# A linear-attention and SwiGLU kernel: making a third block's basis weights in block 1 beside the weights, and a later block's attention by halves of the heads

## The chip, the cores and the metric

The kernel runs on one core of a Trainium2 chip. The core has five engines that run side by side and meet at semaphores: TensorE (PE, matrix products into PSUM; its weight loads are listed as PEld), VectorE (DVE), ScalarE (ACT), GpSimd (POOL) and SyncE (SP, which here only issues DMAs). The metric is the device time in microseconds (us). Each engine works through its own list of instructions in a fixed order; an instruction that waits holds up all behind it on its engine.

## The reference

q, k and v have 8 batches, 8 heads, 576 positions and 64 columns in float32.

```python
kv  = einsum('bhsd,bhse->bhde', k, v)          # no softmax
out = einsum('bhsd,bhde->bhse', q, kv)
rms = sqrt(mean(out*out, axis=-1) + 1e-6)
x   = (out / rms * g_norm)                     # -> 4608 tokens x 512
g   = x @ w_gate                               # 512 x 1536
h   = g * (1 / (1 + exp(-g))) * (x @ w_val)
y   = h @ w_out                                # 1536 x 512
```

## The kernel before, in words

**Blocks.** The 4608 tokens are cut into nine blocks of 512. A block crosses from one batch to the next, since a batch has 576 positions. Block 0 is computed plainly while the weights come in. Blocks 1 and 2 run alone, with a scheme of seven products in place of eight (Winograd's form of Strassen's). Blocks 3 to 8 run in three pairs with the scheme applied twice, so that each weight tile of a pair is replaced by 7 x 7 basis blocks ("leaves") of 128 x 128. These are kept in the DRAM tensor `w` and streamed back for each pair.

**Products.** An up-projection of blocks 1 and 2 has six units (`Up`, index j), each with the products 1, 5, 6, 2, 7, 4, 3. They are called (j, p) here. Unit j runs (j,1), (j,5), then the last two of the unit before, (j-1,4) and (j-1,3), then (j,6), (j,2), (j,7). Each is eight instructions at L650 in the trace. Products 1, 6, 7 and 4 accumulate in one PSUM tile `b`, 5 and 3 in `c`, 2 in `a`. After 1, 6 and 7 ScalarE copies `b` out (L666, L670, L700). After 2, 7 and 3 VectorE adds `a` or `c` to such a copy (L696, L704, L717, listed at L130); (j,3) writes into `c` and so comes after the add of (j,7). GpSimd makes the operand tiles `t` (L131) and multiplies into `h` (L132), and VectorE makes sums of `h` (`h_sums`). The down-projection (`Down`) then runs the products in the order 1, 6, 5, 7, 2, 4, 3 with 24 instructions each.

**Leaves.** In block 1 the three tiles that GpSimd made for a unit are turned into leaves (`leaf_steps`, L908): per tile four VectorE operations and two sends to `w` by SP (L915). The other four outer tiles, that is the raw weights `wg[j]` and `wv[j]`, are turned into leaves in block 2, two groups of tiles per unit with four VectorE operations and two sends each. This is done in place, so it can only begin after the unit's last product, at `p == 3`; the last unit's are done in block 2's down-projection (`latest`, L1091). `make` (L1043) runs up to four such steps after each product in block 1 and two in block 2.

**Attention ahead.** While block 2 is computed, block 3's attention is made beside its products, and block 4's is begun (`ahead`, L1209). A pair (j, p) names the product after which a step is placed:

- (0,7): the k^T v products of block 3 (`visit`; L368), into two PSUM tiles `m`. Block 3's q loads are queued (32 DMAs at L331, sent five after each product), and half of block 4's k and v loads (L310).
- (1,7): half of block 4's k^T v. Then VectorE transposes q (`turn_q`, L384), in two operations.
- (2,5) and (3,5): the products q (k^T v) of one half of block 3 each (`heads`, L423), into the two tiles `m`. A half is two of the four tiles of tokens, with all heads, and so it needs both transposed halves of q, since a transposed half has half of the heads. Behind each half come ScalarE's squares, VectorE's sums and root, and VectorE's scaling (L132), which frees `m`. At (2,5) block 4's q loads are queued.
- (3,7): the second half of block 4's k^T v. At (4,5) sixteen DMAs move the transposed x into its place (`place_x`, L511, eight by SP and eight by ScalarE's queue); at (5,1) ScalarE multiplies it by the gain (`gain_x`, L518); at (5,5) VectorE makes four sums of x (`sum_steps`).

**What sets the order.** A scheduler at build time orders each engine's list. In block 2, PE's list and, in the up-projection, VectorE's are held in program order (`in_order`, L1284 and L1309); ScalarE's, GpSimd's and SP's are not, except that the sends of leaves stay in order. DMAs share eight completion counters in turn, and each waits for the one before it on its counter, whichever queue that was on. A tile pool's buffer is given out again when all that used it are done: four buffers for loads (`ld`), five for `r`, nine for `t`, two for `m`.

Of the kernel before, what the change touches and what calls it, by code (L numbers as in the profile page):

```python
# [8 lines left out]
F32 = mybir.dt.float32  # L9
# [5 lines left out]
P = 128  # L15
# [3 lines left out]
def kernel(  # L19
# [41 lines left out]
    nc = tc.nc  # L61

    B, H, S, D = q.shape
# [166 lines left out]
    class Att:  # L230


        def __init__(self, n):
            self.n = n

            self.cut, half = divmod(n, 2)
            self.split = half * D
            self.ps, self.z = {}, None
            self.q, self.k, self.v, self.room = [], {}, {}, None
            self.halves = []  # L240
            self.quarters = n > 0
            slot = (n - PAIRED) % 2
            self.x, self.xi = (x_alone, xi_alone) if n < PAIRED else (x_slots[slot], xi_slots[slot])
            self.homes = {}
# [160 lines left out]
        def chores(self, i):  # L405
# [5 lines left out]
            for u in range(2):  # L411
                yield lambda u=u: self.scale(i, (u,))

        def heads(self, i, pairs, pools=None):
            if pools:
                self.ps[i] = [pool.tile([P, 2, NS, D], F32, name=pool.name[0]) for pool in pools]
            for t in range(2):
                for j in pairs:
                    for b, _, p0, p1 in self.parts(2 * i + t):
                        for p in range(p0, p1, D):  # L420
                            for u in range(2):
                                rows = slice(u * D, (u + 1) * D)
                                self.multiplied = nc.tensor.matmul(  # L423
                                    self.ps[i][u][p : p + D, t, j, :],
                                    lhsT=self.qt[rows, 2 * i + t, j, p : p + D], rhs=kvs[b % 3][rows, j, :],
                                    start=True, stop=True,
                                )

        def squares(self, i, us=(0, 1)):
            if self.z is None or 0 < self.n < TURNED:  # L430
                self.z = st_pool.tile([P, 2, 2, 2, NS], F32, name="z")
            if i == 0 and us[0] == 0:
                self.sq = self.place("sq").rearrange("p f (t j d) -> p f t j d", t=2, j=NS)
# [16 lines left out]
        def guess(self, i, k):  # L450

            z = self.z[:, i : i + k]
            nc.vector.tensor_scalar(out=z, in0=z, scalar1=1.0 / D, scalar2=eps, op0=OP.mult, op1=OP.add)
            self.y, a = (st_pool.tile([P, 2, 2, 2, NS], F32, name=x) for x in "ya")
# [15 lines left out]
        def scale(self, i, us=(0, 1)):  # L470
            if i == 0 and us[0] == 0:
                self.xts = self.place("xts").rearrange("p (i t) (j u d) -> p i t j u d", i=2, j=NS, u=2)
            for u in us:
                y = self.y[:, i, u].unsqueeze(3).to_broadcast([P, 2, NS, D])
                self.scaled = mul(nc.vector, self.xts[:, i, :, :, u], self.ps[i][u], y)

        def turn_x(self, i):
            xt = self.xts[:, i].rearrange("p t j u d -> p t j (u d)")
# [193 lines left out]
    class Up(Quad):  # L672
# [51 lines left out]
        def multiply(self, p):  # L724
            super().multiply(p)
            ffn = self.ffn
            if ffn.n == 1:
                if p == 5:
                    self.leaf_room = ring().rearrange("p f (s c) -> p (f s) c", c=P)
                if p in (5, 7, 4):  # L730
                    at = 3 * (5, 7, 4).index(p)
                    ffn.making.extend(leaf_steps(self.j, [(self.w[p].unsqueeze(1), (p,))], self.leaf_room[:, at:]))
            if ffn.n == 2 and p == 3:
                room = xi_alone.rearrange("p a b c -> p (a b) c")
                halves = lambda t: t[self.j].rearrange("p (o i) c -> p o i c", o=2)
                steps = leaf_steps(self.j, [(halves(wg), (1, 2)), (halves(wv), (6, 3))], room)
                if self.j < NP - 1:
                    ffn.making.extend(steps)
                else:
                    ffn.latest.extend(steps)  # L740

    class Inner:

# [159 lines left out]
    def t_tile(key=None):  # L903

        stream.held.append(key)
        return t_pool.tile([P, 2, 2 * P], F32, name="t")

    def leaf_steps(j, sources, room):  # L908


        i = 0

        def send(os, ps, src):
            dst = stream.dram[:, j, steps_of(OUTERS, os), steps_of(INNERS, ps)].rearrange("p o i c -> p o (i c)")
            tc.keep_in_program_order(nc.sync.dma_start(out=dst, in_=src))  # L915

        for t, os in sources:
            n = len(os)
            t = t.rearrange("p o i (e c) -> p o i e c", e=2)
            b11, t2_, b22 = t[:, :, 0, 0], t[:, :, 0, 1], t[:, :, 1, 1]  # L920
            to = room[:, i : i + 3 * n].rearrange("p (o r) c -> p o r c", r=3)
            yield lambda b22=b22, t2_=t2_: sub(nc.vector, t2_, b22, t2_)
            yield lambda b11=b11, t2_=t2_: add(nc.vector, t2_, t2_, b11)
            yield lambda t=t, t2_=t2_, to=to, n=n: sub(
                nc.vector, to[:, :, 1:3], t[:, :, 1], t2_.unsqueeze(2).to_broadcast([P, n, 2, P])
            )
            yield lambda t=t, os=os: send(os, (1, 6, 2, 3), t.rearrange("p o i e c -> p o (i e c)"))
            yield lambda b11=b11, t2_=t2_, to=to: sub(nc.vector, to[:, :, 0], b11, t2_)
            yield lambda to=to, os=os: send(os, (7, 4, 5), to.rearrange("p o r c -> p o (r c)"))
            i += 3 * n  # L930

    class Down(Quad):
        def __init__(self, ffn):
# [87 lines left out]
    class Ffn:  # L1021
        def __init__(self, n, att):
            self.n, self.att = n, att
            self.h = h_alone if n < PAIRED else h_slots[(n - PAIRED) % 2]
            self.ps, self.leaf_room, self.ended, self.owed = {}, None, None, None

            self.making, self.latest = [], []
            self.chores, self.sends = [], []
            self.visited = None

# [11 lines left out]

        def make(self, count):  # L1043
            for _ in range(count):
                if self.making:
                    self.making.pop(0)()

        def up(self, fill):

# [4 lines left out]
            for i, this in enumerate(units):  # L1054
                if i + 1 < len(units):
                    units[i + 1].prepare()
                for unit, p in this.sequence(last):
                    if unit:
                        visited, self.visited = self.visited, None
                        with tc.issue_after(visited.ins) if visited else ExitStack():  # L1060
                            unit.multiply(p)
                        self.make(4 if self.n == 1 else 2)
# [11 lines left out]
        def down(self, nxt, then={}):  # L1074
# [3 lines left out]
            for p in (1, 6, 5, 7, 2, 4, 3) if 5 in fill else (1, 5, 6, 7, 2, 4, 3):  # L1078
# [9 lines left out]
                    fill[p]()  # L1088
                if p in then:
                    then[p]()  # L1090
                if p == 5 and self.latest:  # L1091

                    with tc.issue_after(nxt.scaled.ins), tc.issue_after(nxt.placed.ins):
                        for step in self.latest:
                            step()
                if p == 1:

# [110 lines left out]

    def ahead(ffn, att, then):  # L1209

        def load(att):
            for i in range(2):
                ffn.sends += att.quarter_steps(i, (0, 1), (nc.sync,))

        def visits():
            visit(ffn, att, (0, 1))
            load(att)
            then.load_kv(0)

        def turn():  # L1220
            visit(ffn, then, (0,), True)
            ffn.chores += [lambda: att.turn_q(0), lambda: att.turn_q(1), lambda: then.load_kv(1)]

        def half(i):
            with tc.issue_after(ffn.multiplied.ins):
# [3 lines left out]
            if i:  # L1229
                ffn.chores += att.turn_steps()  # L1230

        def last():
            visit(ffn, then, (1,), True)
# [138 lines left out]
```

## Time and profile before

| | us |
|---|---|
| median of 3 runs | 1032.51 |
| lowest, highest | 1031.76, 1033.65 |
| the profiled execution | 1033.4 |
| its span on the core | 1031.6 |
| PE busy | 1000.9 (97% of the span) |
| DVE, POOL, ACT busy | 653.2, 366.0, 232.5 |
| block 1, up-projection, from | 155.9 to 232.3 |
| block 2, up-projection, from | 269.9 to 369.0 |

Times in rows of the profile are from the start of the span. A row of the timeline gives start, duration, engine, line, operation, what is written and read, the count, and in brackets how long the engine stood idle before it and what ended that. A row of PE's waits gives the engine and what it waited to do, whose result it waited for, the total, how often, and the longest. The line L130, L131 or L132 is that of a small helper for adding, subtracting or multiplying, so that such rows are told apart by their tiles. "Granted clock" is TensorE's clock as a share of its full speed.

### The profile page before, as it was taken

The page shows a single profiled execution, that of the slowest core. Times are in us where ns is not written, and L with a number is a line of the kernel's source. Part 1 is how long each engine was busy: PE and PEld are TensorE (multiplying, and loading weights), DVE is VectorE, ACT ScalarE, POOL GpSimd, SP SyncE. Part 2 cuts the span into 40 slices and gives each one's busy share as a digit, 9 for nine tenths or more (in the row PEclk, how much of TensorE's full clock was granted, in tenths as well). Part 3 has the DMA queues.
Part 4 walks back from the last instruction along what each step waited for, and adds up shares of the span by engine and source line. Part 5 has one row for each costly group of instructions (what it writes and reads, how often), then busy time and mean ns, then how long its engine had stood idle before and what let it go on. Part 6 is the DMA issues. An engine that isn't in the chain of part 4 may idle for free.

```text
span 1031.6 us, 17068 instructions
## 1 busy us (share of the span) xinstructions
PE 1000.9 (97%) x6506; PEld 835.1 (81%) x6506; DVE 653.2 (63%) x1118; ACT 232.5 (23%) x367; POOL 366.0 (35%) x290
## 2 busy tenths in 40 slices
PE   5999999999968999999999999999999999999998
PEld 4544688888857888888888888888888888888887
DVE  2999685664348697666666755666777566666211
ACT  2766112221212221111211212212112122121100
POOL 0000262527224140444565102555651026546600
PEclk9999999999989899999999999999999999999999
DMA  8689643463166668586752364667412654543011
GB/s 216 200 263 266 131 79 110 135 202 71 59 158 164 170 171 237 143 236 155 167 148 53 101 144 148 164 168 181 112 22 61 143 146 148 156 142 100 1 42 41
DMA packets 247763, 143.23 MB, mean 139 GB/s; under 512 B 149121, under 2 KB 226945, under 8 KB 247681
## 3 DMA queue, kind: packets, MB, share of 16 engines
q1 hardware_dynamic: 212736, 137.67, 49.1%
q10 hardware_dynamic: 34880, 4.46, 2.7%
q8 instruction: 52, 0.85, 0.4%
q14 instruction: 31, 0.25, 0.1%
q0 software_dynamic: 64, 0.00, 0.0%
HBM read 104.99 MB, written 28.70 MB: 130 GB/s over the span
## 4 chain that ended last, share of the span: by engine, by line
PE 90%; DMA 3%; DVE 2%; SPq 2%; ACT 1%; issue 1%; POOL 1%; ACTq 0%; DVEq 0%; POOLq 0%
PE b L650 24%; PE b L801 21%; PE c L650 11%; PE c L801 11%; PE a L650 6%; PE a L801 5%; PE b L1110 4%; PE c L1110 4%; PE m L423 2%; PE m L368 1%; SPq L331 1%; DMA arena<-in_v_dram 1%; POOL t L131 1%; DMA arena<-r 1%; DMA ld<-in_v_dram 1%
## 5 line engine op out<-in xcount | busy, mean ns | idle before, releaser
L801 PE MATMUL b<-arena,t 128*128 128x256 f32 x1008 | 244.5, 381 | 0.0
L801 PEld LDWEIGHTS b<-arena,t 128*128 128x128 f32 x1008 | 190.0, 190 | 29.6 <-DVE r L130 2.4
L130 POOL TENSOR_TENSOR r<-r 128x256 f32<-128x256 f32 (+1 forms) x90 | 94.7, 1053 | 247.1 <-DMA t<-w 150.1
L130 DVE TENSOR_TENSOR r<-c,r 128x512 f32<-128x512 f32 (+1 forms) x170 | 104.8, 625 | 114.9 <-PE c L801 40.9
L130 DVE TENSOR_TENSOR r<-b,r 128x512 f32<-128x512 f32 (+1 forms) x234 | 139.0, 607 | 60.8 <-PE b L801 55.4
L132 POOL TENSOR_TENSOR arena<-r 128x1024 f32<-128x1024 f32 (+1 forms) x54 | 102.0, 1904 | 108.1 <-DVE r L130 64.2
L131 POOL TENSOR_TENSOR t<-wo 128x512 f32<-128x512 f32 x54 | 75.8, 1424 | 181.2 <-DVE wo L130 105.5
L130 DVE TENSOR_TENSOR r<-a,r 128x512 f32<-128x512 f32 x93 | 59.3, 638 | 122.9 <-PE a L650 87.4
L801 PE MATMUL c<-arena,t 128*128 128x256 f32 x504 | 122.5, 379 | 0.8 <-ACT r L815 0.8
L131 DVE TENSOR_TENSOR arena<-arena 128x512 f32<-128x512 f32 (+3 forms) x102 | 100.9, 998 | 15.1 <-PE b L650 13.8
L801 PEld LDWEIGHTS c<-arena,t 128*128 128x128 f32 x504 | 95.6, 190 | 14.5 <-ACT r L815 1.2
L650 PE MATMUL b<-wo,arena 128*128 128x256 f32 x432 | 98.0, 381 | 0.1
L650 PE MATMUL b<-t,arena 128*128 128x256 f32 x432 | 96.4, 379 | 1.4 <-POOL s L130 0.7
L650 PEld LDWEIGHTS b<-t,arena 128*128 128x128 f32 x432 | 81.9, 190 | 13.2 <-POOL s L130 1.1
L650 PEld LDWEIGHTS b<-wo,arena 128*128 128x128 f32 x432 | 81.3, 190 | 12.0 <-DVE arena L132 0.9
L815 ACT COPY r<-b 128x512 f32<-128x512 f32 x54 | 31.7, 586 | 191.3 <-PE b L801 191.3
L131 POOL TENSOR_TENSOR t<-arena 128x512 f32<-128x512 f32 x36 | 48.8, 1366 | 68.6 <-PE b L650 26.4
L801 PE MATMUL a<-arena,t 128*128 128x256 f32 x252 | 66.1, 379 | 0.0
L801 PEld LDWEIGHTS a<-arena,t 128*128 128x128 f32 x252 | 47.9, 190 | 6.5
L650 PE MATMUL c<-t,s 128*128 128x256 f32 x216 | 48.1, 379 | 0.0
L650 PE MATMUL a<-wo,arena 128*128 128x256 f32 x216 | 48.1, 379 | 0.0
L650 PE MATMUL c<-wo,arena 128*128 128x256 f32 x216 | 48.1, 379 | 0.0
(102 smaller groups left out, 1224.0 us busy)
## 6 DMA issues: line engine op xcount, KB each, us to landing
t<-w SPq DMA_DIRECT2D x180, 256.0 KB, 3.2
out_dram<-r SPq DMA_DIRECT2D x17, 512.0 KB, 2.8
ld<-in_k_dram SPq DMA_DIRECT2D x26, 288.0 KB, 4.4
ld<-in_v_dram SPq DMA_DIRECT2D x26, 288.0 KB, 5.5
t<-w SPq DMA_DIRECT2D x54, 128.0 KB, 2.2
ld<-in_moe_w_gate_dram SPq DMA_DIRECT2D x12, 512.0 KB, 4.9
ld<-in_moe_w_val_dram SPq DMA_DIRECT2D x12, 512.0 KB, 4.6
ld<-in_moe_w_out_dram SPq DMA_DIRECT2D x12, 512.0 KB, 4.8
```

The lines of the kernel that those rows point to most:

```text
L130: add = lambda e, o, a, b: e.tensor_tensor(out=o, in0=a, in1=b, op=OP.add)
L131: sub = lambda e, o, a, b: e.tensor_tensor(out=o, in0=a, in1=b, op=OP.subtract)
L132: mul = lambda e, o, a, b: e.tensor_tensor(out=o, in0=a, in1=b, op=OP.mult)
L331: queue.dma_start(out=to[32 * r : 32 * (r + 1), j, g0:g1], in_=q[b, 4 * i + 2 * j + h, s0 : s0 + 32 * (g1 - g0), 32 * d : 32 * (d + 1)].re ...
L368: self.positions = nc.tensor.matmul(self.kv_ps[r][u * D : (u + 1) * D, g, :], lhsT=k[:, u, c, :], rhs=v[:, u, c, :], start=(c == 0), stop= ...
L423: self.multiplied = nc.tensor.matmul(self.ps[i][u][p : p + D, t, j, :], lhsT=self.qt[rows, 2 * i + t, j, p : p + D], rhs=kvs[b % 3][rows, ...
L650: self.ffn.multiplied = nc.tensor.matmul(banks[e][:, e], lhsT=lhsT, rhs=rhs, start=first and i == 0 and (e == 0 or banks[0] is not banks[1 ...
L801: self.ffn.multiplied = nc.tensor.matmul(ps[:, i], lhsT=stream.use(self.ffn.n, self.j, o, p), rhs=self.operand(o, p), start=first and i == ...
L815: nc.scalar.copy(out=dst, in_=ps)
L1110: nc.tensor.matmul(t, lhsT=w[f // 2][:, i, P * (f % 2) : P * (f % 2 + 1)], rhs=x[:, i, of], start=(i == 0), stop=(i == NS - 1),)
```

## The change

It has three parts.

1. The leaves of the raw weights are made in block 1, into room of their own (`xi_alone`), and no longer in place (`kept_steps`). Per unit there are again two groups of four VectorE operations. They stand in a list `later`, from which `make` takes when the list of the other leaves is empty; the last two units' groups run in block 1's down-projection. Since the weights stay as they are, leaves that are equal to a raw weight are sent from it (`raw_steps`): for units 0 and 1 in block 1, for units 2 to 5 in block 2. Each group has now two sends of made leaves and two of raw ones, four in place of two.
2. Block 3's attention is made by halves of the heads (`by_heads`, `places`): a half has all four tiles of tokens and four heads, those of one half of q.
3. The steps of `ahead` move: block 3's k^T v from (0,7) to (0,1), its q loads with it, the q transposes to (1,6) and (2,6), the halves to (2,1) and (3,1), block 4's q loads to (2,7) with the 16 raw sends behind them, `place_x` to (4,1), `gain_x` to (4,6) and the sums to (4,7).

```diff
+            self.by_heads = n == PAIRED
+            self.shape = (T, 2) if self.by_heads else (2, NS)
...
+        def places(self, i, pairs):
+            if self.by_heads:
+                return [(t, j, t, 2 * i + j) for t in range(T) for j in range(2)]
+            return [(t, j, 2 * i + t, j) for t in range(2) for j in pairs]
...
-            if ffn.n == 2 and p == 3:
-                room = xi_alone.rearrange("p a b c -> p (a b) c")
-                halves = lambda t: t[self.j].rearrange("p (o i) c -> p o i c", o=2)
-                steps = leaf_steps(self.j, [(halves(wg), (1, 2)), (halves(wv), (6, 3))], room)
-                if self.j < NP - 1:
-                    ffn.making.extend(steps)
-                else:
-                    ffn.latest.extend(steps)
+                if p == 3:
+                    if ffn.leaf_room is None:
+                        ffn.leaf_room = xi_alone.rearrange("p a b c -> p (a b) c")
+                    steps = lambda room: kept_steps(self.j, room)
+                    if self.j < NP - 2:
+                        ffn.later.extend(steps(ffn.leaf_room))
+                    else:
+                        ffn.latest.append(steps)
...
+    def kept(j):
+        halves = lambda t: t[j].rearrange("p (o i) (e c) -> p o i e c", o=2, e=2)
+        return [(halves(wg), (1, 2)), (halves(wv), (6, 3))]
+
+    def raw_steps(j):
+        for t, os in kept(j):
+            yield lambda t=t, os=os: send_leaf(j, os, (1,), t[:, :, 0, 0])
+            yield lambda t=t, os=os: send_leaf(j, os, (2, 3), t[:, :, 1].rearrange("p o e c -> p o (e c)"))
+
+    def kept_steps(j, room):
+        for i, (t, os) in enumerate(kept(j)):
+            b11, b12, b22 = t[:, :, 0, 0], t[:, :, 0, 1], t[:, :, 1, 1]
+            to = room[:, 8 * i : 8 * (i + 1)].rearrange("p (o r) c -> p o r c", r=4)
+            t2_ = to[:, :, 0]
+            yield lambda b22=b22, b12=b12, t2_=t2_: sub(nc.vector, t2_, b22, b12)
+            yield lambda b11=b11, t2_=t2_: add(nc.vector, t2_, t2_, b11)
+            yield lambda t=t, t2_=t2_, to=to: sub(
+                nc.vector, to[:, :, 2:4], t[:, :, 1], t2_.unsqueeze(2).to_broadcast([P, 2, 2, P])
+            )
+            yield lambda t2_=t2_, os=os: send_leaf(j, os, (6,), t2_)
+            yield lambda b11=b11, t2_=t2_, to=to: sub(nc.vector, to[:, :, 1], b11, t2_)
+            yield lambda to=to, os=os: send_leaf(
+                j, os, (7, 4, 5), to[:, :, 1:4].rearrange("p o r c -> p o (r c)")
+            )
+        if j < 2:
+            yield from raw_steps(j)
...
         def make(self, count):
             for _ in range(count):
-                if self.making:
-                    self.making.pop(0)()
+                steps = self.making or self.later
+                if steps:
+                    steps.pop(0)()
...
-                if p == 5 and self.latest:
+                if p in (5, 7) and self.latest:
                     with tc.issue_after(nxt.scaled.ins), tc.issue_after(nxt.placed.ins):
-                        for step in self.latest:
+                        room = self.leaf_room if p == 5 else ring().rearrange("p f (s c) -> p (f s) c", c=P)
+                        for step in self.latest.pop(0)(room):
                             step()
...
     def ahead(ffn, att, then):
-        def visits():
-            visit(ffn, att, (0, 1))
-            load(att)
-            then.load_kv(0)
+        def first():
+            visit(ffn, att, (0, 1))
+            ffn.sends += [load(att, 0), lambda: then.load_kv(0), load(att, 1)]
...
+        def rest():
+            for i in range(2):
+                load(then, i)()
+            for j in range(2, NP):
+                ffn.sends += raw_steps(j)
+
         return {
-            (0, 7): visits, (1, 7): turn, (2, 5): lambda: (half(0), load(then)), (3, 5): lambda: half(1), (3, 7): last,
-            (4, 5): att.place_x, (5, 1): att.gain_x, (5, 5): lambda: ffn.chores.extend(att.sum_steps()),
+            (0, 1): first, (1, 6): lambda: turn(0), (1, 7): second, (2, 1): lambda: half(0), (2, 6): lambda: turn(1),
+            (2, 7): rest, (3, 1): lambda: half(1), (3, 7): lambda: visit(ffn, then, (1,), True), (4, 1): att.place_x,
+            (4, 6): att.gain_x, (4, 7): lambda: ffn.chores.extend(att.sum_steps()),
         }
```

More of the change, by code (lines that the diff above doesn't have):

```diff
@@ L412, in chores @@
                 yield lambda u=u: self.scale(i, (u,))
+        def places(self, i, pairs):
+            if self.by_heads:
+                return [(t, j, t, 2 * i + j) for t in range(T) for j in range(2)]
+            return [(t, j, 2 * i + t, j) for t in range(2) for j in pairs]
         def heads(self, i, pairs, pools=None):
             if pools:
[L416 to L427, printed above, removed]
+                self.ps[i] = [pool.tile([P, *self.shape, D], F32, name=pool.name[0]) for pool in pools]
+            for t, j, tile_t, head in self.places(i, pairs):
+                for b, _, p0, p1 in self.parts(tile_t):
+                    for p in range(p0, p1, D):
+                        for u in range(2):
+                            rows = slice(u * D, (u + 1) * D)
+                            self.multiplied = nc.tensor.matmul(
+                                self.ps[i][u][p : p + D, t, j, :],
+                                lhsT=self.qt[rows, tile_t, head, p : p + D], rhs=kvs[b % 3][rows, head, :],
+                                start=True, stop=True,
+                            )
         def squares(self, i, us=(0, 1)):
             if self.z is None or 0 < self.n < TURNED:
-                self.z = st_pool.tile([P, 2, 2, 2, NS], F32, name="z")
+                self.z = st_pool.tile([P, 2, 2, *self.shape], F32, name="z")
             if i == 0 and us[0] == 0:
-                self.sq = self.place("sq").rearrange("p f (t j d) -> p f t j d", t=2, j=NS)
+                self.sq = self.place("sq").rearrange("p f (t j d) -> p f t j d", t=self.shape[0], j=self.shape[1])
             for u in us:
@@ L453, in guess @@
             nc.vector.tensor_scalar(out=z, in0=z, scalar1=1.0 / D, scalar2=eps, op0=OP.mult, op1=OP.add)
-            self.y, a = (st_pool.tile([P, 2, 2, 2, NS], F32, name=x) for x in "ya")
+            self.y, a = (st_pool.tile([P, 2, 2, *self.shape], F32, name=x) for x in "ya")
             y, a = self.y[:, i : i + k], a[:, i : i + k]
@@ L473, in scale @@
             for u in us:
-                y = self.y[:, i, u].unsqueeze(3).to_broadcast([P, 2, NS, D])
-                self.scaled = mul(nc.vector, self.xts[:, i, :, :, u], self.ps[i][u], y)
+                y = self.y[:, i, u].unsqueeze(3).to_broadcast([P, *self.shape, D])
+                to = self.xts[:, i, :, :, u]
+                if self.by_heads:
+                    to = self.xts.rearrange("p i t j u d -> p (i t) j u d")[:, :, 2 * i : 2 * i + 2, u]
+                self.scaled = mul(nc.vector, to, self.ps[i][u], y)
         def turn_x(self, i):
@@ L906, in t_tile, with send_leaf @@
         return t_pool.tile([P, 2, 2 * P], F32, name="t")
+    def send_leaf(j, os, ps, src):
+        dst = stream.dram[:, j, steps_of(OUTERS, os), steps_of(INNERS, ps)].rearrange("p o i c -> p o (i c)")
+        tc.keep_in_program_order(nc.sync.dma_start(out=dst, in_=src))
     def leaf_steps(j, sources, room):
         i = 0
-        def send(os, ps, src):
-            dst = stream.dram[:, j, steps_of(OUTERS, os), steps_of(INNERS, ps)].rearrange("p o i c -> p o (i c)")
-            tc.keep_in_program_order(nc.sync.dma_start(out=dst, in_=src))
         for t, os in sources:
@@ L926, in leaf_steps @@
             )
-            yield lambda t=t, os=os: send(os, (1, 6, 2, 3), t.rearrange("p o i e c -> p o (i e c)"))
+            yield lambda t=t, os=os: send_leaf(j, os, (1, 6, 2, 3), t.rearrange("p o i e c -> p o (i e c)"))
             yield lambda b11=b11, t2_=t2_, to=to: sub(nc.vector, to[:, :, 0], b11, t2_)
-            yield lambda to=to, os=os: send(os, (7, 4, 5), to.rearrange("p o r c -> p o (r c)"))
+            yield lambda to=to, os=os: send_leaf(j, os, (7, 4, 5), to.rearrange("p o r c -> p o (r c)"))
             i += 3 * n
+    def kept(j):
[19 more added lines that the diff above has]
+                j, os, (7, 4, 5), to[:, :, 1:4].rearrange("p o r c -> p o (r c)")
+            )
+        if j < 2:
+            yield from raw_steps(j)
     class Down(Quad):
@@ L1025, in __init__ @@
             self.ps, self.leaf_room, self.ended, self.owed = {}, None, None, None
-            self.making, self.latest = [], []
+            self.making, self.later, self.latest = [], [], []
             self.chores, self.sends = [], []
@@ L1061, in up @@
                             unit.multiply(p)
-                        self.make(4 if self.n == 1 else 2)
+                        self.make(4)
                         for steps, most in ((self.chores, 2), (self.sends, 5)):
@@ L1209, in ahead, with load, turn, second @@
     def ahead(ffn, att, then):
-        def load(att):
-            for i in range(2):
-                ffn.sends += att.quarter_steps(i, (0, 1), (nc.sync,))
-        def visits():
+        def load(att, i):
+            return lambda: ffn.sends.extend(att.quarter_steps(i, (0, 1), (nc.sync,)))
+        def first():
             visit(ffn, att, (0, 1))
-            load(att)
-            then.load_kv(0)
-        def turn():
+            ffn.sends += [load(att, 0), lambda: then.load_kv(0), load(att, 1)]
+        def turn(i):
+            ffn.chores.append(lambda: att.turn_q(i))
+        def second():
             visit(ffn, then, (0,), True)
-            ffn.chores += [lambda: att.turn_q(0), lambda: att.turn_q(1), lambda: then.load_kv(1)]
+            ffn.sends.append(lambda: then.load_kv(1))
         def half(i):
@@ L1230, in half @@
                 ffn.chores += att.turn_steps()
-        def last():
-            visit(ffn, then, (1,), True)
+        def rest():
[3 more added lines that the diff above has]
+                ffn.sends += raw_steps(j)
         return {
-            (0, 7): visits, (1, 7): turn, (2, 5): lambda: (half(0), load(then)), (3, 5): lambda: half(1), (3, 7): last,
-            (4, 5): att.place_x, (5, 1): att.gain_x, (5, 5): lambda: ffn.chores.extend(att.sum_steps()),
+            (0, 1): first, (1, 6): lambda: turn(0), (1, 7): second, (2, 1): lambda: half(0), (2, 6): lambda: turn(1),
+            (2, 7): rest, (3, 1): lambda: half(1), (3, 7): lambda: visit(ffn, then, (1,), True), (4, 1): att.place_x,
+            (4, 6): att.gain_x, (4, 7): lambda: ffn.chores.extend(att.sum_steps()),
         }
```

## The prediction, made before the result was known

> **What bounds the kernel now.** I read the page first (TensorE, PE, is busy 97% of the span), then PE's waits, then the stretches in which it waits, then the other engines' rows there. Time can only be won where PE stands still or runs slow. PE's waits, as total, times, longest:
>
> ```profile
> PE m L423 <- DVE r L384: 8.0, 2, 7.4
> PE m L368 <- issue: 3.7, 1, 3.7
> ```
>
> Both lie in block 2. Busy time by stretches (PE, PEld, DVE, ACT, POOL, then the granted clock, DMA share, GB/s): block 1's and block 2's up-projection, and two short stretches inside the second.
>
> ```profile
> 155.90:232.30 76.40, 76.40 (x486) 66.67 (x486) 45.24 (x105) 17.75 (x32) 28.91 (x23) 1.00 0.50 151
> 269.90:369.00 99.10, 86.00 (x754) 73.43 (x753) 58.76 (x105) 22.79 (x42) 30.11 (x23) 0.93 0.58 152
> 303.20:310.10 6.90, 3.60 (x53) 3.12 (x54) 2.83 (x4) 1.08 (x2) 0.00 (x0) 0.51 0.81 234
> 334.00:340.80 6.80, 5.70 (x79) 4.87 (x80) 6.66 (x12) 1.00 (x3) 0.00 (x0) 0.50 0.17 60
> ```
>
> Block 1 runs with no wait; block 2 takes 22.7 us more, of which 4.5 are its longer attention part. Two stalls, and half clock after each, are the target. VectorE (DVE) around them, and around the places that the change touches:
>
> ```profile
> 119.44 1.24 DVE L384 STREAM_TRANSPOSE r<-ld 128x1024 f32<-128x1024 f32 x1
> 121.20 1.25 DVE L384 STREAM_TRANSPOSE r<-ld 128x1024 f32<-128x1024 f32 x1 [0.53 <-DMA ld<-in_q_dram]
> ...
> 138.30 1.75 DVE L131 TENSOR_TENSOR arena<-arena 128x512 f32<-128x512 f32 x1
> ...
> 305.20 1.25 DVE L384 STREAM_TRANSPOSE r<-ld 128x1024 f32<-128x1024 f32 x1 [6.72 <-DMA ld<-in_q_dram]
> ...
> 334.19 1.28 DVE L132 TENSOR_TENSOR r<-m,y 128x512 f32<-128x512 f32 x2
> ...
> 360.00 0.69 DVE L130 TENSOR_TENSOR arena<-arena 128x512 f32<-128x512 f32 x1 [1.92 <-ACT arena L518]
> ```
>
> The first stall is the second q transpose (305.20), late by its loads. The second ends when the scaling (334.19) gives up its m banks to the k^T v products; it comes late because leaf steps stand between it and its squares. Other rows used, of ScalarE, GpSimd, PE and the queues:
>
> ```profile
> 357.79 2.18 ACT L518 ACTIVATE arena<-arena,gain 128x1024 f32<-128x1024 f32 x2
> 137.95 8.59 POOL L131 TENSOR_TENSOR t<-arena 128x512 f32<-128x512 f32 x6 [1.33 <-DVE arena L130]
> 364.93 1.96 PE L650 MATMUL b<-arena,t 128*128 128x256 f32 x8 [0.77 <-ACT r L700]
> 367.15 1.99 PE L650 MATMUL c<-arena 128*128 128x256 f32 x8 [0.26 <-DVE r L130]
> 341.39 7.46 ACTq L511 DMA_DIRECT2D arena<-r  x8
> 330.89 15.24 SPq L915 DMA_DIRECT2D w<-arena  x4
> 283.48 11.97 SPq L331 DMA_DIRECT2D ld<-in_q_dram  x20
> arena<-r SPq DMA_DIRECT2D x64, 64.0 KB, 3.6
> ```
>
> (the last: median us from issue to landing).
>
> **What it removes.** Stalls 0.55 + 7.41 (L423) and 3.71 (L368); of the half-clock stretches half the busy time, 3.60/2 + 5.70/2 = 4.65. Together **16.3 us**, if the new order keeps both away. I walked it at 1.73 us a product. k^T v of block 3 (2.27) now follows product (0,1), ending near 273.9 instead of 280.9. SP sends block 4's k, v (3.4, of which 2.5 after PE lets go), then 16 q loads at 0.6 = 9.6: near 286, landed 2.7 later, 289. The first half needs only this half of q; its transpose stands after (1,2), 291.8 to 293.1, its products after (2,1), 295.9: 2.8 us to spare, 4.6 from the landing. The second half's q lands near 298, its products come at 309. The scaling of the second half ends near 318.9; the k^T v that reuses its banks comes at 320.9. So both stalls go; 48 leaf instructions, 4 for each of 12 groups, are out of DVE's way.
>
> **What it adds before block 2.** One group is sub, add and sub of 256 columns (about 0.44 from start to start in DVE's rows of block 2, as at 323.07 and 323.52) and one sub of 512 (0.6): 1.9 us undisturbed.
> - The built order puts group one at the end of block 0, ahead of both q transposes. Before, they end at 122.45 and PE needs them at 122.72. The second will end at 117.7 + 1.9 + 1.8 + 2.5 = 123.9: PE waits up to 1.2. The first products need only the first transpose: I take **0.9** (0 to 1.3).
> - Group two falls between DVE's 141.7 and PE's a result at 145.8, beside six GpSimd ops. The row: a 512-column DVE op takes 1.75 there against 0.68 alone. The Trainium skill (SBUF — State Buffer, "SBUF: two separate sides") says that a VectorE op with both inputs in SBUF and a GpSimd op that reads SBUF hold one shared port in turn, and the loser blocks for the whole instruction. By undisturbed rows the group ends at 143.6 and costs nothing. By the lock four more turns of 1.5 to 1.7 end near 148; the reading of c behind it then ends at about 151.2, and PE's last product of block 0 overwrites c at 150.75. I take **0.5** (0 to 1.5).
> - Six groups in block 1's up-projection: 11 us, or some 17 with the lock, into 76.4 - 45.2 = 31 free ones. Nearest deadline: the add to c after (5,7), 229.8 against 230.5. Zero; up to 1 if one GpSimd op gets between.
> - Two units' groups in block 1's down-projection: near 248.3 to 260.3, and 263.3 to 269.8. c is read by 263.3 (needed 264.9), the sums of x follow by 271 to 272, needed at 273.9 and 275.6 because k^T v now stands in front. Zero.
> - Sends: 24 more issues at 0.4, 16 of them moved into block 2. In block 1 they delay block 3's k, v to about 236, used at 271.6: zero.
>
> **What it adds in block 2.** SP gets block 4's 32 q loads and 8 raw sends ahead of its half of the move of x (place_x), 8 more raw sends behind it. DMAs share eight counters in turn, each waiting for the one before it on its counter: 330.89 shows four sends held 15 us so. Block 4's ninth second-half q load waits for ScalarE's first move, which waits for DVE's turned x (322.3): SP stands from 313 to 326.8, then 15 issues at 0.4 to 0.6, then eight moves at 0.85, landed at about **344** (last issue 340.4 + 3.6). ScalarE's own eight moves end near 332.5, one waiting on SP in turn; two ScalarE ops behind them make PE wait about 1.1 before (4,7), against 0.28 now (ACT at 349.4): **+0.8** (0 to 2).
>
> The decisive step: the built ScalarE order puts gain_x (2.18) behind the copy of unit 5's product 7; before, it stood two copies earlier. On DVE the four sums of x, which wait for gain_x, stand ahead of three adds, the last of which reads c for unit 5; PE's last up product, (5,3), overwrites c. In before's time: (5,7) ends 364.1, copy to 364.8, gain to 366.9, four sums at 0.605 to 369.3, adds 0.6 + 0.6 + 0.68 to 371.2. PE starts 371.25 instead of 367.15: **+4.1**, an idle of 4.4. x having landed by 344 is 4 us earlier than gain_x's turn, so the queues don't decide.
>
> The clock after it: the row nearest, idle 3.71, gave 6.8 us of half clock, 2.85 lost. The Trainium skill (TensorE: Matmul & The Clock Gate, "The HAM clock gate") halves the clock after one idle window of about 3.4 us and restores it after one busy window, so 1.7 lost. It speaks against the change: now 0.77 and 0.26 sit at this place, harmless. I take the row, **2.9** (0 if the idle straddles two windows, to 3.4).
>
> **Sum.** 16.3 - (0.9 + 0.5 + 0.8 + 4.1 + 2.9) = 7.1 us faster (8.3 by the rule's clock). The profiled execution took 1033.4 (span 1031.6 plus 1.8 around it): it would give 1026.3. The median shown is 0.9 below it: **1025.4**. After block 2 nothing changes.
>
> **Rivals.**
> - Full gain: if the sums don't hold the adds, 1032.5 - 16.3 + 2.2 = 1018.4. For it: place_x lands in time. Against: the static orders.
> - More small waits in blocks 0 and 1 (upper bounds 1.3 + 1.5 + 1, and 2 before (4,7), in place of 2.2): 1029. For it the lock, against it DVE's 31 free us.
> - The change doesn't do what it says: half a q still lands late. It needs 4.6 us more than reckoned before PE waits, 11.7 to eat all: near 1033. Against it: 283.48 shows 0.6 an issue with the same neighbours.
> - Slower: SP's chain of counters. If each of the 23 issues from the held load to the last move waits a landing of its own on average 1.4 us rather than 0.6, x lands after 356 instead of 344. gain_x's turn is at about 348.7; each us beyond adds one to the stall at (5,3), so 355.8 is the point of no gain; 360 gives 1037. For it 15.24 for four sends; against it, the page's eight moves in about 7.
>
> **How the numbers follow.** The likeliest case 0.5 (its own range 1022 to 1028.5), full gain 0.2, more small waits 0.17, no effect 0.07, slower 0.06. A measurement tells 0.2%, 2.1 us, from no change: faster 0.89, same 0.05, slower 0.06. The range 1018 to 1030.4 leaves out the last two and the lower end of the full gain.
>
> **What would show it.** PE's waits: no L386 before the heads of block 3, no 3.7 before its second k^T v; a wait of about 4.4 by (5,3) on DVE, with ScalarE's gain ahead of it, half clock after; 1 us before block 1's heads. Block 2's up-projection near 90 us. Wrong: (5,3) within 1 us of (5,4), or gain_x waiting for SP.

## The result and the profile after

The changed kernel takes 1026.7 us, the median of four runs (1025.7 to 1027.27), against 1032.39 before (1031.76 to 1033.65). The ratio is 0.9942, with a 95% interval of 0.9925 to 0.996, so a gain of 5.7 us that is clear of the noise. The prediction was 1025.4, range 1018 to 1030.4. The profiled run took 1027.02, with a span of 1025.2.

In the new file the lines stand some 2 to 11 further down: products L661 (was L650), heads L431 (L423), k^T v L370 (L368), q transposes L386 (L384), the move of x L522 (L511), gain_x L529 (L518), sends L921 (L915), copies of `b` L677, L681 and L711.

TensorE's waits in the changed kernel (total, times, longest):

```profile
PE c L661 <- DVE r L130: 5.1, 3, 4.6
...
PE b L661 <- issue: 1.3, 1, 1.3
PE b L661 <- POOL arena L132: 1.0, 1, 1.0
PE b L661 <- ACT r L711: 0.8, 1, 0.8
...
PE m L431 <- DVE r L386: 0.3, 1, 0.3
```

Of the 8.0 us for q transposes 0.3 is left (at block 0's end), and the 3.7 before k^T v is gone. In their place stands one wait of 4.6 on VectorE, and waits of 1.3 and 1.0 that the kernel before did not have. By stretches, block 1's and block 2's up-projection, then a short stretch in block 2's end (columns as before: busy time of PE, PEld, DVE, ACT, POOL, then clock, DMA share, GB/s):

```profile
155.90:232.76 76.86, 76.61 (x485) 66.55 (x484) 56.58 (x120) 17.88 (x32) 29.78 (x23) 1.00 0.58 185
273.15:361.14 87.99, 82.62 (x754) 71.02 (x753) 42.27 (x70) 22.74 (x42) 29.09 (x23) 0.98 0.64 144
356.86:363.69 6.83, 6.13 (x14) 4.88 (x15) 3.54 (x7) 0.63 (x1) 3.52 (x3) 0.50 0.45 98
```

Block 2's up-projection fell from 99.1 to 88.0 us and has one stretch of half clock instead of two. VectorE's work moved from block 2 (58.8 to 42.3) to block 1 (45.2 to 56.6). How the wait of 4.6 comes about is seen in three engines' rows at block 2's end. VectorE:

```profile
352.97 0.69 DVE L130 TENSOR_TENSOR arena<-arena 128x512 f32<-128x512 f32 x1 [10.37 <-DMA ld<-in_k_dram]
353.57 2.14 DVE L131 TENSOR_TENSOR arena<-arena 128x512 f32<-128x512 f32 x3
355.63 0.68 DVE L130 TENSOR_TENSOR r<-c,r 128x512 f32<-128x512 f32 x1
356.23 0.68 DVE L130 TENSOR_TENSOR r<-a,r 128x512 f32<-128x512 f32 x1
356.83 0.68 DVE L130 TENSOR_TENSOR r<-c,r 128x512 f32<-128x512 f32 x1
```

ScalarE, SyncE's half of the move of x, and TensorE:

```profile
350.26 0.59 ACT L711 COPY r<-b 128x512 f32<-128x512 f32 x1 [2.87 <-PE b L661]
350.75 2.19 ACT L529 ACTIVATE arena<-arena,gain 128x1024 f32<-128x1024 f32 x2
...
337.85 5.40 SPq L522 DMA_DIRECT2D arena<-r  x8
...
351.00 1.97 PE L661 MATMUL b<-arena,t 128*128 128x256 f32 x8 [0.77 <-ACT r L711]
357.56 3.78 PE L661 MATMUL c<-arena 128*128 128x256 f32 x8 [4.60 <-DVE r L130]
361.14 6.61 PE L661 MATMUL b<-wo,arena 128*128 128x256 f32 x24
```

VectorE stood for 10.37 us before the sums of x. The row names a DMA, but that DMA is only what ended at about that time. The sums began 0.03 after gain_x ended (350.75 + 2.19 = 352.94), and gain_x had stood behind the copy of (5,7). The move of x had been issued by 343.25; with the 3.5 that such transfers take here from issue to landing (the median), it landed near 346.8, which is an estimate. Behind the four sums came three adds, and the last of them freed `c` for (5,3) at 357.5.

The whole difference of the two profiled runs, by the starts of TensorE's products:

| stretch | before | after | difference | predicted |
|---|---|---|---|---|
| start to block 0's first down product | 117.34 | 116.25 | -1.1 | 0 |
| to its second | 7.40 | 7.98 | +0.6 | +0.9 |
| to its last | 26.00 | 26.39 | +0.4 | +0.5 |
| to block 1's first down product | 81.52 | 82.14 | +0.6 | 0 |
| to its second | 6.44 | 7.66 | +1.2 | 0 |
| to its third | 5.28 | 6.83 | +1.6 | 0 |
| to its last | 20.72 | 20.72 | 0 | 0 |
| to block 2's second down product | 111.58 | 101.72 | -9.9 | -8.5 |
| to the end of the span | 655.3 | 655.5 | +0.2 | 0 |

So the total was near for three reasons: block 2 gained 1.4 more than predicted, block 1 lost 3.4 that were not predicted, and the profiled runs differ by 1.1 at the start. That 1.1 is there by 21 us already, while the first loads come in and long before the first instruction that the change adds (116.86, on VectorE). Seven of the experiments' profiles have 116.0 to 116.5 in this row and one has 115.5. Of before there is one profile, of a run (1033.4) that was itself 1.0 above its kernel's median; so most of the 1.1 is likely that run's; this was not shown.

That these differences nearly cancel is luck. The parts that were foreseen came close, but with block 1's 3.4 in its sum the same prediction would have been 3.7 us faster, not 7.1.

### The profile page after: what moved, and what is told of

It is laid out like the page before. It is cut to its first block, busy times and chain, and to the rows that moved or that the text cites. A ratio compares the mean times of both kernels' runs of the same rounds, so it can differ in the third digit from the quotient of the medians.

```text
span 1025.2 us, 17084 instructions
## 1 busy us (share of the span) xinstructions
PE 999.9 (98%) x6506; PEld 833.1 (81%) x6506; DVE 666.3 (65%) x1118; ACT 232.5 (23%) x367; POOL 367.6 (36%) x290
## 4 chain that ended last, share of the span: by engine, by line
PE 81%; DVE 10%; DMA 4%; SPq 1%; ACT 1%; POOL 1%; issue 1%; DVEq 0%; ACTq 0%; POOLq 0%
PE b L661 22%; PE b L812 22%; PE c L661 12%; PE c L812 11%; PE a L661 6%; PE a L812 5%; DVE arena L131 2%; PE m L431 1%; DVE r L190 1%; PE m L370 1%; SPq L333 1%; DVE arena L199 1%; DMA arena<-in_v_dram 1%; DMA ld<-in_v_dram 1%; DVE r L184 1%
## 5 line engine op out<-in xcount | busy, mean ns | idle before, releaser
L131 DVE TENSOR_TENSOR arena<-arena 128x512 f32<-128x512 f32 (+3 forms) x96 | 103.7, 1090 | 22.6 <-PE b L661 14.9
L661 PE MATMUL b<-wo,arena 128*128 128x256 f32 x432 | 99.8, 385 | 2.3 <-issue 1.3
L661 PE MATMUL b<-t,arena 128*128 128x256 f32 x432 | 96.4, 379 | 1.4 <-POOL s L130 0.7
L661 PEld LDWEIGHTS b<-wo,arena 128*128 128x128 f32 x432 | 82.1, 192 | 15.5 <-issue 1.7
L661 PEld LDWEIGHTS b<-t,arena 128*128 128x128 f32 x432 | 81.9, 190 | 13.2 <-POOL s L130 1.1
L131 POOL TENSOR_TENSOR t<-arena 128x512 f32<-128x512 f32 x36 | 51.4, 1438 | 59.0 <-PE c L661 20.2
L661 PE MATMUL c<-wo,arena 128*128 128x256 f32 x216 | 48.2, 379 | 0.2 <-DVE r L130 0.2
L661 PE MATMUL c<-t,s 128*128 128x256 f32 x216 | 48.1, 379 | 0.0
L661 PE MATMUL a<-wo,arena 128*128 128x256 f32 x216 | 48.1, 379 | 0.0
```

The costliest lines, as they stand in the source:

```text
L131: sub = lambda e, o, a, b: e.tensor_tensor(out=o, in0=a, in1=b, op=OP.subtract)
L661: self.ffn.multiplied = nc.tensor.matmul(banks[e][:, e], lhsT=lhsT, rhs=rhs, start=first and i == 0 and (e == 0 or banks[0] is not banks[1 ...
```

## The experiments

All times are medians, and each run was measured against the kernel before on the same chip (1032.5 to 1033.0 there). The same table of starts serves as the reading of each. Where two runs differ by one or two microseconds, their intervals overlap; what an edit removes is then read from these starts, in one profile of each run.

**The sums of x behind the adds.** First the cause of the wait of 4.6.

```diff
-            (4, 6): att.gain_x, (4, 7): lambda: ffn.chores.extend(att.sum_steps()),
+            (4, 6): att.gain_x,
...
                 ffn.up(ahead(ffn, nxt, blocks[PAIRED + 1]))
+                nxt.sums()
```

> The changed kernel with one thing moved: the four sums of x stand on VectorE behind the adds of block 2's last product instead of ahead of three adds of unit 5. My theory (the sums, waiting for gain_x, hold the add that frees c for (5,3)): PE's wait before (5,3) falls from 4.6 to under 0.5 us, the stretch of half clock behind it goes, 1026.7 - 4.3 - 3.0 = 1019.4. Rival (gain_x on ScalarE itself, by holding the copies behind it, is what delays (5,3)): a wait of 2 us or more stays and the time is above 1022.

Measured: 1019.29 us, ratio 0.987 (0.9855 to 0.9885). Product (5,3) follows (5,4) by 1.80 us, TensorE's clock is whole to the end, and the stretch to block 2's second down product is 93.85 instead of 101.72. ScalarE and TensorE of this run:

```profile
350.55 0.59 ACT L711 COPY r<-b 128x512 f32<-128x512 f32 x1 [2.87 <-PE b L661]
351.03 0.64 ACT L714 ACTIVATE r<-r 128x512 f32<-128x512 f32 x1
351.56 2.18 ACT L529 ACTIVATE arena<-arena,gain 128x1024 f32<-128x1024 f32 x2
...
351.28 1.97 PE L661 MATMUL b<-arena,t 128*128 128x256 f32 x8 [0.77 <-ACT r L711]
353.08 1.89 PE L661 MATMUL c<-arena 128*128 128x256 f32 x8
```

gain_x is even later than in the changed kernel, and TensorE does not wait for it. So it was the place of the sums in VectorE's order that made a late gain_x cost anything.

**gain_x ahead of the copy.** The other end of the same chain. VectorE's order is left as it was.

```diff
+            gained = blocks[PAIRED].gained if self.ffn.n == 2 and self.j == NP - 1 else None
+            with tc.issue_after(gained.ins) if gained else ExitStack():
-            copied = nc.scalar.copy(out=self.u3, in_=self.ps["b"])
+                copied = nc.scalar.copy(out=self.u3, in_=self.ps["b"])
```

> The changed kernel with gain_x put ahead of the copy of (5,7) on ScalarE, VectorE's order as it was. My theory (gain_x's place is late, x has long landed): gain_x starts near 347.4, the sums end near 352.1, three adds by 354.1, PE's wait before (5,3) is about 1.2 us and no half clock follows: 1026.7 - 3.5 - 3.0 = 1020.2. Rival (SyncE's chain of sends and loads makes x land late, the order of ScalarE only hides it): gain_x waits for the move of x until 350 or later, the copy of (5,7) stands behind it, and the time is 1024 or more.

Measured: 1020.63 us, ratio 0.9884 (0.9869 to 0.9899). ScalarE and TensorE:

```profile
347.03 0.59 ACT L681 COPY r<-b 128x512 f32<-128x512 f32 x1 [2.86 <-PE b L661]
347.51 2.19 ACT L529 ACTIVATE arena<-arena,gain 128x1024 f32<-128x1024 f32 x2
...
354.32 1.99 PE L661 MATMUL c<-arena 128*128 128x256 f32 x8 [1.15 <-DVE r L130]
```

gain_x started right behind the copy before it, so x was there by 347.5. The rival with SyncE's chain falls, for this order: gain_x began at 350.75 in the changed kernel, so the queues had about 3 us in hand.

**The two hoisted leaf groups held back.** `added` is VectorE's add of (j,7), kept in that function as `self.ffn.added`.

```diff
                 if steps:
-                    steps.pop(0)()
+                    with tc.issue_after(self.added.ins) if steps is self.later else ExitStack():
+                        steps.pop(0)()
```

> The changed kernel with the two leaf groups that the built order has at the end of block 0 held back into block 1's up-projection (only VectorE's order and one place on SyncE differ). My theory (these two groups cost 0.6 before the heads of block 1 and 0.5 before block 0's last down product): from the first down product of block 0 to the first up product of block 1 it takes 38.6 us again instead of 39.65, and 1025.6 in all; block 1's end, whose VectorE gets eight more instructions earlier in the block, loses the same 3.3. Rival (block 1's end is late for want of VectorE's time): it loses 1 to 3 us more there, and the time is 1027 to 1029.

Measured: 1025.94 us, ratio 0.9934 (0.9918 to 0.9951). The two stretches of block 0's end are 7.40 and 26.00, exactly those of before. Block 1 keeps its loss (82.12, 7.54, 6.98), although VectorE has eight more instructions there: what it loses at its end is not a matter of VectorE's time over the whole block.

**The leaves alone.** Block 3's attention goes back to whole heads and to the order of before.

```diff
-            self.by_heads = n == PAIRED
+            self.by_heads = False
...
-            (0, 1): first, (1, 6): lambda: turn(0), (1, 7): second, (2, 1): lambda: half(0), (2, 6): lambda: turn(1),
-            (2, 7): rest, (3, 1): lambda: half(1), (3, 7): lambda: visit(ffn, then, (1,), True), (4, 1): att.place_x,
-            (4, 6): att.gain_x, (4, 7): lambda: ffn.chores.extend(att.sum_steps()),
+            (0, 7): visits, (1, 7): turn, (2, 5): rest, (3, 5): lambda: half(1), (3, 7): last,
+            (4, 5): att.place_x, (5, 1): att.gain_x, (5, 5): lambda: ffn.chores.extend(att.sum_steps()),
```

> The changed kernel with the leaf groups of all units made in block 1 as there, but block 3's attention in block 2 as the kernel before has it (whole heads by token halves, the same order of loads, heads, gain_x and sums). My theory: the stall before the second k^T v product (3.7) and its half clock (2.85) go, since no leaf step stands ahead of the scaling; the stall at the second q transpose (7.4) with its half clock stays; blocks 0 and 1 cost 1.1 + 3.3 more: 1032.4 - 6.6 + 4.4 = 1030.2. Rival (the second stall came from the late q as well): both stalls stay and the time is 1036 or more.

Measured: 1031.03 us, ratio 0.9983 (0.9976 to 0.999). TensorE's waits:

```profile
PE m L431 <- DVE r L386: 6.5, 1, 6.5
...
PE b L661 <- ACT r L681: 2.9, 2, 2.2
PE b L661 <- issue: 1.8, 1, 1.8
PE b L661 <- POOL arena L132: 1.0, 1, 1.0
```

The wait before k^T v is down to 0.3 and the late q transpose stays, as expected; block 1's waits are there as well, so they come with the leaves. A wait of 2.2 is new: ScalarE's half of the move of x takes 337.44 to 346.33 here, and a copy of `b` stands behind it. So the leaves' part, taken alone, is worth 0.2%, under 2 us. The attention's part brings the rest on top of the leaves; alone, without them, it was not run.

**Block 3's k and v later.** From here on the kernel with the sums behind the adds (1019.29) is the base. SyncE now issues the eight loads behind the move of x in block 1's down-projection, and no longer ahead of its first product.

```diff
             nxt.turn()
-            for g in range(2):
-                blocks[PAIRED].load_kv(g)
...
+        def load_kv():
+            with tc.issue_after(nxt.placed.ins):
+                for g in range(2):
+                    blocks[PAIRED].load_kv(g)
+
-        ffn.down(nxt, {7: inner_sums} if n == 2 else {})
+        ffn.down(nxt, [{}, {5: load_kv}, {7: inner_sums}][n])
```

> The kernel of the run with the sums later (1019.3), and block 3's eight loads of k and v held on SyncE behind the move of x in block 1's down-projection, instead of ahead of its first product; VectorE's order and PE's are the same but for one pair. My theory (the loads and the leaf sends fill the DMA engines from 232 to 244 us, and a piece of PE's own instructions, landed at 242.9 to 243.9, comes late behind them: PE stands 1.4 us in the middle of the second down product with nothing it waits for): the DMA share there falls, the piece lands earlier, that stall goes: 1017.9. The stall of 0.8 before it, which is VectorE's, stays. Rival (the stall in the middle of the product belongs to that place in PE's instructions, whatever the DMAs do): 1.4 us stay and the time is 1019.3.

Measured: 1017.58 us, ratio 0.9855 (0.9836 to 0.9873). The stretch to block 1's third down product is 5.28 again, against 6.96 in the base; the wait in the first down product stays (7.66). The stretch from 240 to 244 us, in the changed kernel and then in this run:

```profile
240.00:244.00 4.00, 3.92 (x51) 3.12 (x39) 3.93 (x7) 1.80 (x4) 3.61 (x2) 1.00 1.05 289
```

```profile
240.00:244.00 4.00, 4.00 (x49) 3.52 (x41) 3.93 (x7) 1.75 (x4) 3.57 (x2) 1.00 0.14 47
```

The engines' work is the same; the DMA engines go from full (share 1.05; 1.04 in the base) to nearly idle (0.14).

**Three units' groups in the down-projection.**

```diff
-                    if self.j < NP - 2:
+                    if self.j < NP - 3:
...
-                if p in (5, 7) and self.latest:
+                if p in (5, 7, 2) and self.latest:
```

> The kernel of the run with the sums later (1019.3), with the leaf groups of three units instead of two made in block 1's down-projection: one group less on VectorE ahead of the last adds of block 1's up-projection. My theory (VectorE, held by the late q transposes, runs behind from 227 to 241 us, and the add that frees c and the last product of h are late): PE's waits of 0.3 before (5,3) and 0.8 in the first down product go, the stall in the second down product stays or shrinks: 1018.2. Rival (the third group in the down-projection is then late itself, at the reading of c before the last down product or at the sums of x): 1019 to 1021.

Measured: 1017.8 us, ratio 0.986 (0.9837 to 0.9884). To block 1's first down product it takes 81.62 and to its second 6.44, as before the change but for 0.1. Of the stall in the second product 0.95 is left (6.23). VectorE in this run:

```profile
224.98 2.37 DVE L386 STREAM_TRANSPOSE r<-ld 128x1024 f32<-128x1024 f32 x2 [2.04 <-DMA w<-r]
...
232.90 0.68 DVE L130 TENSOR_TENSOR r<-c,r 128x512 f32<-128x512 f32 x1
```

The q transposes still come late, after a wait of 2.04, but the add on which the last product of `h` waits (232.90; 233.09 in the kernel before, 235.14 in the changed one) stands in time again. So one unit's groups less are enough, with the transposes as late as before. Whether transposes in time would have been enough with all the groups in place was not run.

**The whole of q again.** By token halves, with the early loads and products kept.

```diff
-            self.by_heads = n == PAIRED
+            self.by_heads = False
...
-            (1, 7): second, (2, 1): lambda: half(0), (2, 6): lambda: turn(1),
+            (1, 7): lambda: (second(), turn(1)), (2, 1): lambda: half(0),
```

> The kernel of the run with the sums later (1019.3), with block 3's attention by token halves again, so that the first half needs both q transposes; the loads, the leaf groups and the places of the products stay. My theory (half a q is what the by-heads order saves: the second half's last load is issued at 298.1 and lands near 300.8, its transpose ends near 302.1, PE is ready for the heads at 299.4): a wait of 2.7 us at the second q transpose before the first half's products and perhaps half clock behind it: 1022 to 1025. Rival (issuing the loads one product run earlier is enough): no wait there, 1019.3.

Measured: 1020.48 us, ratio 0.9882 (0.9864 to 0.99): 1.2 above its base, half of what was expected, and without half clock. VectorE and TensorE:

```profile
300.02 1.25 DVE L386 STREAM_TRANSPOSE r<-ld 128x1024 f32<-128x1024 f32 x1 [1.19 <-DMA ld<-in_q_dram]
...
301.32 0.93 PE L431 MATMUL m<-kv,r 64*64 64x64 f32 x48 [1.21 <-DVE r L386]
```

The second half of q was there at 300.0 rather than 300.8. TensorE came to the heads at 299.7, ran sixteen of their instructions, and waited from 300.1 to 301.3. Of the 7.4 us of the first stall the early loads remove some six; the halves of the heads remove the last 1.2.

**Four edits together.** The sums behind the adds, the groups held back, three units' groups in the down-projection, and k and v later: the diffs above.

> Four edits of the runs before together on the changed kernel: the sums behind the adds, the two hoisted leaf groups held in block 1, three units' leaf groups in block 1's down-projection, block 3's k and v behind the move of x. My theory (each removes a wait of its own on TensorE, so the gains add up): block 0's end 7.40 + 26.0, block 1 81.6 + 6.44 + 5.28 + 20.7, block 2 86.6 + 7.3, with the unchanged parts a span of 1012.9 and 1014.8 in all. Rival (they share one cause, VectorE's or the queues' time in block 1, and taking all away only moves the wait): 1016.5 to 1018.

Measured: 1015.77 us (1014.7 to 1016.33), ratio 0.9835 (0.9822 to 0.9848), span 1012.9. The stretches are 7.40, 26.00, 81.52, 6.47, 5.28, 20.72 and 93.87. TensorE's waits beyond the start:

```profile
PE b L661 <- ACT r L711: 0.8, 1, 0.8
PE c L812 <- ACT r L826: 0.8, 1, 0.8
PE b L661 <- POOL s L130: 0.7, 1, 0.7
PE b L661 <- ACT r L681: 0.7, 1, 0.7
```

The span is the one expected to a tenth; the profiled run took 1014.7, and the median is 1.0 above the expected 1014.8. The gains add up (7.4, 0.8, 1.5 and 1.7 one by one, 11.4 in sum; 10.9 together), so the waits were in the main separate. This kernel is 11 us faster than the changed one and 17 faster than the one before.

## Why the prediction was right

**The removal of 16.3 held.** Both stalls and both stretches of half clock are gone. Without the new wait, block 2 up to its second down product takes 93.85 against 111.58, which is 17.7. The 1.4 beyond the sum's 16.3 holds the waits of 0.28 and 0.26 at block 2's end, which the sum left standing; the rest of it was not traced further. The half q had 2.8 us to spare in the prediction; its transpose ends at 296.7 and the heads begin at 299.5, which is 2.8, with both ends 3.6 later. What the prediction gave to the halves of the heads, though, is mostly the earlier loading: only 1.2 of it needs the halves.

**The decisive step, +4.1, held: 4.3.** From the start of (5,4) to that of (5,3) it takes 6.56 instead of 2.22. The chain is the one written down: the copy of (5,7), gain_x, four sums, three adds. Broken at either end it lets go (1019.3 and 1020.6). The sums are the tie that matters: gain_x may come late if they stand behind the adds.

**The half clock, +2.9, held: 3.1.** The profile gives 6.83 us at clock 0.50, with 6.13 busy, so 3.07 lost. By the Trainium skill (TensorE: Matmul & The Clock Gate, "The HAM clock gate") the clock comes back after one busy window of about 3.4 us, from which the prediction had worked out 1.7. Here the trace differs: 6.8 us again, as in the row of before.

**Block 0's end, +0.9 and +0.5: 0.6 and 0.4.** Holding the groups back restores 7.40 and 26.00, so both terms are theirs. The first is not one number: the six other runs that leave the groups there have 7.67 to 8.74 in this row, and 26.4 in the next. Whether the second term is the lock on the shared port, which the prediction took from the Trainium skill (SBUF — State Buffer, "SBUF: two separate sides"), or the mere length of the group was not separated; beside GpSimd's subtractions VectorE's 512-column operations took 1.6 here too, against 0.68 alone.

**+0.8 before (4,7) did not come.** ScalarE's eight moves ended at 334.10, and the copy of (4,6) behind them went at 334.73 while TensorE was busy with (4,2). In the run with all edits, where TensorE is 4.5 us earlier, there is no wait either. Only in the leaves-alone run, where the same move comes behind 16 sends on SyncE, does it cost 2.2.

**The step that failed is block 1, put at nothing in two places: "Zero; up to 1" for the groups, and "zero" for block 3's k and v.** Together they cost 3.4. The first is 1.8 of it, up to block 1's second down product, and the second the 1.6 behind that, though one unit's groups less took 0.7 off that part too (6.96 to 6.23).

First, the prediction took the add of (5,7) as the nearest deadline. It was met but for 0.25 (TensorE's wait before (5,3)). The one that cost more is one add later: the add after (5,3), on which GpSimd's last product of `h` and then the last four instructions of the first down product wait. VectorE, GpSimd and TensorE of the changed kernel there:

```profile
225.53 2.37 DVE L386 STREAM_TRANSPOSE r<-ld 128x1024 f32<-128x1024 f32 x2 [2.04 <-DMA w<-r]
...
235.14 0.68 DVE L130 TENSOR_TENSOR r<-c,r 128x512 f32<-128x512 f32 x1
...
235.91 1.37 POOL L132 TENSOR_TENSOR arena<-r 128x512 f32<-128x512 f32 x1 [3.24 <-DVE r L130]
...
237.33 1.13 PE L661 MATMUL b<-wo,arena 128*128 128x256 f32 x4 [0.96 <-POOL arena L132]
245.21 2.21 PE L661 MATMUL b<-wo,arena 128*128 128x256 f32 x9 [1.28 <-issue]
```

In the kernel before, the add at 235.14 stood two microseconds earlier:

```profile
233.09 0.68 DVE L130 TENSOR_TENSOR r<-c,r 128x512 f32<-128x512 f32 x1
```

The row of the q transposes names what they waited for, a send of leaves out of `r`, the pool that they write into; why that send was late was not traced. The share of VectorE over the block was no guide: 56.6 of 76.9 us leaves 20 free, and yet it was late in the last ten. One unit's groups less there remove this part.

Second, the delay of block 3's k and v "to about 236, used at 271.6: zero" looked only at who uses them. They then ran together with the leaf sends, and TensorE stood from about 243.9 to 245.2 in the middle of a product (last section).

**The rivals.** "More small waits" was right in block 1 and wrong before (4,7), and came beside the likeliest case rather than instead of it. "Full gain" is what the first experiment shows: 1018.4 predicted for sums that don't hold the adds, 1019.3 measured with block 1's loss still in it. SyncE's chain was some 9 us from its point of no gain: the move landed near 346.8, by the estimate above, against 355.8.

## What to carry to other kernels

Work moved to an engine with free time has to meet the deadlines of the last few microseconds of the stage, not its average: list every add that frees a buffer, to the last one. In a fixed order, a waiting instruction is as expensive as what stands behind it; moving four sums behind three adds was worth more than the whole change. A transfer that is moved has two costs, when it lands and what else is under way when it runs.

## What the runs showed of the hardware that was not expected

**TensorE stood in the middle of a product while the DMA engines were full, most likely for want of its own instructions.** The page lists a DMA queue of instructions:

```profile
q8 instruction: 52, 0.85, 0.3%
```

These are 52 pieces of 16 KB, 65 bytes for each of TensorE's 13,012 matmuls and weight loads; that the queue is TensorE's is inferred from this count. The trace has one of them at 242.9 to 244.0 in the changed kernel, and the product goes on at 245.2. TensorE's order up to there is the same in all kernels, so the same piece can be followed: it starts at 236.3 before, 238.2 with k and v later, 235.5 with all four edits, and no stall in those three; at 239.7 with three units' groups in the down-projection, with what is left of the stall. In the other runs, with the whole stall, it starts at 242.0 to 243.1. All seven runs that stall stop at the same place, behind the 15th of the product's 24 instructions. From 240 to 244 us the DMA share was 1.05 in the changed kernel and 0.02 before:

```profile
240.00:244.00 4.00, 4.00 (x21) 3.51 (x20) 3.52 (x14) 0.00 (x0) 0.97 (x1) 1.00 0.02 4
```

The wait list calls the stall "issue", since TensorE waited for nothing that the profile shows. That the full DMA engines bring the late piece and the stall is shown by the run with k and v later; that this piece is what TensorE lacked follows from the times and the place alone.

**The half clock comes in steps of 3.41 us, and where they fall sets the price.** The same idle of 4.60 us at the same place was followed by this stretch in the run with the groups held back:

```profile
354.28:361.11 6.83, 4.41 (x10) 3.53 (x11) 4.70 (x7) 0.63 (x1) 2.68 (x2) 0.50 0.75 166
```

It began 2.4 us before the idle ended, and in the changed kernel 0.7, so only 4.41 us of work ran at half speed instead of 6.13: 2.2 lost instead of 3.1. And a wait of 2.22 us, shorter than the idle window of about 3.4 us that the Trainium skill names (TensorE: Matmul & The Clock Gate, "The HAM clock gate"), was followed by one step in the leaves-alone run:

```profile
348.90:352.31 3.41, 3.41 (x10) 2.68 (x9) 1.55 (x4) 1.11 (x2) 0.00 (x0) 0.50 0.72 102
```

Between the first loads and the last products, waits of 1.8 and less had none behind them, in any of the traces. The five of 3.7 and more had two steps each (7.41 and 3.71 before the change, 4.60 in the changed kernel and with the groups held back, 6.52 with the leaves alone).
